# One core, transformer block: phi from v + 1, key sums out of G, normalized rows made by ScalarE

## The chip, the cores and the metric

The kernel runs on one core of a Trainium2 chip. The metric is device time in microseconds (us), the median of several executions. A core has TensorE (PE, the matrix engine), VectorE (DVE), ScalarE (ACT), GpSimd (POOL) and SyncE (SP), which here only starts DMAs. Each engine runs its own instructions in the order of the program and waits for the others through semaphores.

## The reference

The input x has 2048 rows of 512 numbers, all in float32.

```python
xn = layernorm(x)                                   # mean and variance of each row
q, k, v = split(xn @ wqkv)                          # 32 heads of 16
phi = lambda t: where(t > 0, t + 1, exp(t)) + 1e-6
pq, pk = phi(q), phi(k)
kv = einsum("bhsd,bhse->bhde", pk, v)               # per head 16 x 16
z = einsum("bhsd->bhd", pk)                         # per head 16: pk summed over all rows
o = einsum("bhqd,bhde->bhqe", pq, kv) / (einsum("bhqd,bhd->bhq", pq, z) + 1e-6)
s = o @ wo
g = silu((gelu(x @ w_gate) * (x @ w_up)) @ w_down)  # 1792 hidden columns; from x here: xn is not used
out = x + s * g
```

In the kernel the FFN and the attention read transposed operands that are made from the same 16 blocks of 128 rows.

## The kernel before

**Number format.** A float32 product is made of three TensorE passes over a high and a low half (`split`: ScalarE casts the high half, VectorE or GpSimd subtracts it to get the low one). The large products use a two by two scheme with seven products (names X, Y, Z in the attention, FX, FY, FZ and dX, dY, dZ in the FFN). One TensorE instruction is a 128x128 weight load and a 128x512 product.

**Stages.** The first stage takes the 16 blocks of x in eight pairs n = 0 to 7, `tokens[n]`. For a block, VectorE makes mean and variance (`bn_stats`, `bn_aggr`), GpSimd the reciprocal root (`rstd`, L557), then `xn` is made. For pairs 0 to 5 (`n < TX`, TX = 6) VectorE makes it (L573, `TENSOR_SCALAR`) and TensorE transposes it into PSUM (`pt`, L643). For pairs 6 and 7 ScalarE makes it (L565), it goes to DRAM (`xn_d`) and comes back laid out so (`xq`) that VectorE can transpose it (L617, `STREAM_TRANSPOSE`). Then come k and q of the block: `plain` products for pairs 0 and 1, the seven products for the others. `phi` (L703 to L713) is relu of -v and exp on ScalarE, and a VectorE operation. G = pk^T xn is summed over all blocks in four PSUM banks (`gps`), and v is never made: kv is G times the v columns of `wqkv` (`pkv`). The sum z of pk is kept by GpSimd (`zacc`, L722, one addition for each block) and summed over partitions by two TensorE products with ones (`pz`, L933); ScalarE copies it to `zq` (L940).

The second stage is the FFN in two halves of seven steps, each with the work on q's denominators and on q's transposes (`den`, `turn`) beside it. At the end stand the products `sps` of attention and output weights, and for each tile a VectorE product with silu's result, an addition of x, and a DMA out (`out_tile`). The last of these tiles is cut into two halves of 256 columns, each with its own product and DMA.

**What sets the order.** All operations are recorded (`do`), and the list `ORDER` gives the sequence in which they are issued, over all engines. It is one long list of numbers, made ahead of time; nothing is decided at run time. Tiles live in numbered places, so an operation that writes one waits for the readers of what was there.

**Idle products.** Twelve products `warm` of a constant tile stand ahead of everything on TensorE (`WARM`), and two more beside the first transposes.

Lines of the profile: L442 is TensorE's sum of passes, L398 and L400 a copy or cast on ScalarE or VectorE, L404 a two-operand operation on VectorE or GpSimd, L394 every DMA. Names tell these apart.

Of the kernel before, what the change touches and what calls it, by code (L numbers as in the profile page):

```python
# [288 lines left out]
def pool(n):  # L289
    return 0.18 + 0.0021 * n  # L290
# [3 lines left out]
def kernel(  # L294
# [246 lines left out]
    def load_next():  # L541
        if xq:
            load_x(xq.pop(0))

    xns = {}

    def ln(*ts):
        n = len(ts)
# [910 lines left out]
```

## Time and profile before

| what | before |
|---|---|
| median of 3 runs | 567.49 us (566.92 to 567.54) |
| the profiled execution | 566.9 us, span 564.8 us |
| PE busy | 557.8 us, 99% |
| DVE / ACT / POOL busy | 493.2 us / 360.8 us / 253.1 us |
| granted TensorE clock, mean | 0.999 |

The span runs from the first to the last instruction; 2.1 us of the profiled execution lie outside it. The ends of products are modelled by the profile, so a busy TensorE is told better by the distance of its starts.

### The profile page before, as it was taken

What the parts mean: (1) busy time and instruction counts of PE and PEld (TensorE: products, weight loads), DVE (VectorE), ACT (ScalarE), POOL (GpSimd) and SP (SyncE); (2) the same over time, 40 slices, a digit from 0 to 9 for tenths busy, and PEclk for the clock granted to TensorE, in tenths of its full rate; (3) what the DMA queues carried; (4) which work ended last, traced back from release to release, by engine and by line L of the source; (5) the groups of instructions that cost most, each with busy time, mean ns of one, the idle gap of its engine ahead of it and who ended that gap; (6) DMA issues with size and microseconds to landing.
All of it is one profiled execution on the core that took longest, in us unless ns stands there. A gap on an engine that the chain in (4) does not pass through costs nothing.

```text
span 564.8 us, 7902 instructions
## 1 busy us (share of the span) xinstructions
PE 557.8 (99%) x2630; PEld 487.0 (86%) x2630; DVE 493.2 (87%) x774; ACT 360.8 (64%) x668; POOL 253.1 (45%) x237
## 2 busy tenths in 40 slices
PE   8999999999999999999999999999999999999997
PEld 6888888888888888888888888888888888888886
DVE  7999999987798999999888776774889989898997
ACT  5987898877677876564536467867555636354730
POOL 4656677757786876431251940430413212314200
PEclk9999999999999999999999999999999999999999
DMA  7378967879978668158867998696757475778776
GB/s 266 104 217 273 274 203 233 255 223 322 352 241 300 240 234 339 43 201 311 265 233 216 389 339 335 239 344 254 243 187 242 173 247 194 233 228 286 239 247 239
DMA packets 78952, 141.29 MB, mean 250 GB/s; under 512 B 4672, under 2 KB 47680, under 8 KB 74944
## 3 DMA queue, kind: packets, MB, share of 16 engines
q1 hardware_dynamic: 78912, 140.79, 72.9%
q8 instruction: 21, 0.34, 0.2%
q14 instruction: 19, 0.16, 0.1%
HBM read 87.82 MB, written 52.95 MB: 249 GB/s over the span
## 4 chain that ended last, share of the span: by engine, by line
PE 91%; DVE 5%; DMA 2%; issue 1%; SPq 1%; ACT 0%; DVEq 0%; ACTq 0%
PE FX L442 26%; PE FZ L442 13%; PE dX L442 12%; PE gps L442 7%; PE FY L442 6%; PE dY L442 6%; PE X L442 6%; PE sps L442 4%; PE dZ L442 3%; PE Z L442 3%; PE q L442 2%; PE k L442 2%; PE Y L442 1%; DVE acc L1119 1%; PE pt L643 1%; DMA wk<-in_A_wqkv 1%
## 5 line engine op out<-in xcount | busy, mean ns | idle before, releaser
L442 PE MATMUL FX<-Xh,w 128*128 128x512 f32 x448 | 125.4, 379 | 0.0
L442 PEld LDWEIGHTS FX<-Xh,w 128*128 128x128 f32 x448 | 84.7, 189 | 12.0
L404 POOL TENSOR_TENSOR sums<-draw 128x256 f32<-128x256 f32 x28 | 26.5, 951 | 109.6 <-DVE dl L404 56.3
L1165 POOL TENSOR_TENSOR h<-h,g 128x512 f32<-128x512 f32 x28 | 39.5, 1411 | 65.9 <-DVE h L404 64.2
L442 PE MATMUL FX<-Xl,w 128*128 128x512 f32 x224 | 66.0, 379 | 0.0
L442 PE MATMUL FZ<-Xh,w 128*128 128x512 f32 x224 | 64.4, 379 | 0.0
L398 ACT COPY dY<-dX 128x512 f32<-128x512 f32 x56 | 32.1, 573 | 46.2 <-DVE acc L1119 28.4
L398 ACT COPY fu<-FX 128x512 f32<-128x512 f32 x56 | 32.7, 585 | 23.3 <-PE FX L442 19.4
L442 PEld LDWEIGHTS FX<-Xl,w 128*128 128x128 f32 x224 | 42.3, 189 | 6.0
L442 PEld LDWEIGHTS FZ<-Xh,w 128*128 128x128 f32 x224 | 42.3, 189 | 6.0
L398 ACT CAST hfh<-sums 128x512 fp32r<-128x512 f32 x56 | 34.5, 619 | 14.3 <-DVE sums L404 14.3
L442 PE MATMUL dX<-hfh,dh 128*128 128x512 f32 x112 | 41.9, 380 | 0.1
L442 PE MATMUL dX<-hfl,dh 128*128 128x512 f32 x112 | 41.5, 380 | 0.0
L442 PE MATMUL dX<-hfh,dl 128*128 128x512 f32 x112 | 41.0, 379 | 0.0
L1119 DVE TENSOR_TENSOR acc<-acc,dY 128x512 f32<-128x512 f32 x48 | 32.7, 681 | 8.9 <-PE dY L442 8.7
L404 DVE TENSOR_TENSOR hfl<-sums,hfh 128x512 fp32r<-128x512 f32 x56 | 40.2, 728 | 0.1
L404 POOL TENSOR_TENSOR tmp<-raw 128x256 f32<-128x256 f32 x28 | 29.1, 1049 | 20.1 <-DVE we L404 10.6
L1119 DVE TENSOR_TENSOR acc<-acc,dX 128x512 f32<-128x512 f32 x48 | 32.7, 683 | 5.5 <-PE dX L442 5.2
L960 POOL TENSOR_TENSOR qz<-qz,zq 128x512 f32<-128x512 f32 x16 | 23.3, 1456 | 23.1 <-DMA qz<-q_d 18.3
L442 PE MATMUL FY<-Xh,w 128*128 128x512 f32 x112 | 33.1, 379 | 0.0
L442 PE MATMUL FZ<-Xl,w 128*128 128x512 f32 x112 | 33.0, 379 | 0.0
L404 DVE TENSOR_TENSOR hfl<-h,hfh 128x512 fp32r<-128x512 f32 x42 | 32.2, 774 | 0.6 <-ACT hfh L398 0.6
(222 smaller groups left out, 1517.7 us busy)
## 6 DMA issues: line engine op xcount, KB each, us to landing
w<-w_d SPq DMA_DIRECT2D x17, 1792.0 KB, 7.9
w_d<-w SPq DMA_DIRECT2D x11, 1792.0 KB, 8.8
draw<-in_B_w_down SPq DMA_DIRECT2D x14, 512.0 KB, 4.0
w_d<-we SPq DMA_DIRECT2D x18, 256.0 KB, 2.2
x<-in_A_x SPq DMA_DIRECT2D x16, 256.0 KB, 3.3
q_d<-qp SPq DMA_DIRECT2D x16, 256.0 KB, 3.7
qz<-q_d SPq DMA_DIRECT2D x16, 256.0 KB, 3.1
q<-q_d SPq DMA_DIRECT2D x16, 256.0 KB, 3.8
```

What stands on the lines that cost most here:

```text
L398: do("ACT", act(n, src.psum), lambda o, i: nc.scalar.copy(o, i), dst, src, name=name)
L404: do(eng, c, lambda o, p, q: getattr(e, f"tensor_{op}")(o, p, q), dst, a, b, name=name)
L442: nc.tensor.matmul(o if r is None else o[:, r], a, turned(b), start=first, stop=made == self.passes[r], skip_group_check=self.on or r is n ...
L643: nc.tensor.transpose(o[:, k, :], a[:, j * P:(j + 1) * P], b)
L960: do("POOL", pool(D), lambda o, z: nc.gpsimd.tensor_mul(o, o, z.unsqueeze(1).to_broadcast([P, KT, P])), rows_of(q), zq, name="u")
L1119: do("DVE", dve(D), lambda o, i: nc.vector.tensor_add(o, o, i), o, ps, name="acc")
L1165: do("POOL", pool(NC), lambda o, i: nc.gpsimd.tensor_mul(o, o, i), h, g, name="h")
```

## The change

- **v + 1.** Where VectorE adds two partial products (`added`), it now adds 1 as well (`c` = v + 1). `phi` of such a tile is exp(c - 1) on ScalarE and max(min(exp, 1), c) on VectorE: one ScalarE operation instead of two, for 12 of the 32 tiles.
- **z.** VectorE writes 1 into the first column of each block of xn, once its transpose has been taken. Row 0 of G is then the sum of pk. It goes to DRAM (`z_d`), and four DMAs bring it to `zq`. `zacc` with its 16 additions, the products `pz` and ScalarE's copies are gone. As a row of xn sums to zero, the lost column is put back through the weights: row 0 of the v columns (`w0`) is subtracted from all of them, two 128x512 tiles on GpSimd and two on VectorE.
- **xn.** `TX` goes from 6 to 4: pairs 4 and 5 go through DRAM as 6 and 7 do. For pairs 1 to 3 (`XA`) ScalarE makes xn, which TensorE transposes as before. VectorE makes only that of pair 0.
- **Idle products.** Sixteen instead of twelve ahead of everything.
- **ORDER** is a new list.

```diff
-    988, 5, 0, 4, 7, 2, 10, 8, 11, 12, 9, 17, 6, 1, 18, 24, 16, 19, 20, 15, 28, 25, 13, 21, 29, 56, 62, 61, 63, 65, 116, 14, 57, 75, 117, 58, 118, 67,
...
-WARM = 12, 2
+WARM = 16,2
...
+    z_d = dram_view([1, D], "z_d")
...
+    neg_one = tile_in("sm", "no", [P, 1], F32, "neg_one")
+    do("DVE", 0.1, lambda o: nc.vector.memset(o, -1.0), neg_one, port=False)
...
-    TX = 6
+    TX = 4
...
+    XA = [(1, 5), (2, 6), (3, 7)]
...
+        if ts in XA:
+            nb = little("nb", f"nb{ts[0]}", [P, n])
+            do("DVE", 0.11, lambda o, i, r: nc.vector.scalar_tensor_tensor(o, i, -1.0, r, op0=ALU.mult, op1=ALU.mult),
+               nb, mv[:, :, 0], rstd)
         for i, t in enumerate(ts):
+            if ts in XA:
+                xns[t] = U("xn", range(4, 9), f"xn{t}")
+                v = xns[t].map(lambda ap: ap.rearrange("p (g q d) -> p q g d", g=KT, d=32))
+                do("ACT", 0.72, lambda o, i, r, b: nc.scalar.activation(o, i, AF.Identity, bias=b, scale=r),
+                   v, xs.pop(t).map(lambda ap: ap.rearrange("p (q g d) -> p q g d", q=KT, d=32)), rstd[:, i:i + 1], nb[:, i:i + 1], name=f"xn{t}")
+                xns[t] = xns[t], v
+                continue
...
+        do("DVE", 0.1, lambda o: nc.vector.memset(o, 1.0), (x[0] if isinstance(x, tuple) else x)[:, 0:1], name="one", port=False)
...
-        tt("DVE", "add", c, e, ps, D, name)
+        do("DVE", 0.6, lambda o, i, j: nc.vector.scalar_tensor_tensor(o, i, 1.0, j, op0=ALU.add, op1=ALU.add), c, ps, e, name=name)
...
+        if not v.psum:
+            do("ACT", act(D), lambda o, i, b: nc.scalar.activation(o, i, AF.Exp, bias=b), r, v, neg_one, name="exp")
+            p0 = U("p", range(24, 28), f"{nm}p{t}")
+            do("DVE", 0.6, lambda o, i, j: nc.vector.scalar_tensor_tensor(o, i, 1.0, j, op0=ALU.min, op1=ALU.max),
+               p0, r, v, name="phi")
+            return p0
...
-        do("POOL", pool(D), lambda o, i: nc.gpsimd.tensor_add(o, o, i), zacc, p0, name="zacc")
...
-    do("PE", 2 * PASS, run_z, pz, ones_r, *zs, key="z")
...
-    do("ACT", 0.7, turn_z, zq, pz, name="zb")
+    dma(z_d(0, slice(None)), GT[0][0:1], 2)
+    for k in range(KT):
+        dma(zq[32 * k:32 * k + 32].map(lambda ap: ap.rearrange("p (g d) -> p g d", d=32)),
+            z_d(0, slice(None)).map(lambda ap, k=k: ap.rearrange("o (g q d) -> o q g d", q=KT, d=32)[:, k].to_broadcast([32, KT, 32])), 16)
...
+    w0 = tile_in("up", 29, [P, D], F32, "w0")
+    dma(w0, ext(wqkv[0:1, 2 * D:3 * D].to_broadcast([P, D])), 256)
+    for c in range(KT):
+        tt("DVE" if c % 2 else "POOL", "sub", wv[c], wv[c], w0, D, "wv")
```

**VectorE at the start of the program.** `st` is a block's statistics, `mv` its mean and variance, `ve` the variance plus a constant. Before:

```order
L552 BN_STATS st_128<-x_97 128x6
L464 MEMSET neg_half 128x1
L553 BN_AGGR mv_133<-st_128 128x2
L555 TENSOR_SCALAR ve_139<-mv_133 128x1
L573 TENSOR_SCALAR xn_148<-x_97,mv_133,rstd_141 128x4x4x32
L552 BN_STATS st_152<-x_121 128x6
```

Now, with the second block's statistics ahead of the first block's xn:

```order
L554 BN_STATS st_133<-x_99 128x6
L555 BN_AGGR mv_136<-st_133 128x2
L557 TENSOR_SCALAR ve_141<-mv_136 128x1
L554 BN_STATS st_152<-x_125 128x6
L586 TENSOR_SCALAR xn_154<-x_99,mv_136,rstd_143 128x4x4x32
L555 BN_AGGR mv_157<-st_152 128x2
```

The block that these statistics read is the fourth DMA of the program, before and now.

**ScalarE at the start of the program**, from the first transposed block on. `kq` are the high halves of weights, `Xh` those of x, `wk` and `wq` the weights as they come from DRAM. Before:

```order
L398 CAST Xh_163<-pt_154 128x2x128 x2
L398 CAST kq_135<-wk_119 128x512
L398 CAST kq_135<-wk_113 128x512
L398 CAST b_0_207<-pt_196 128x256
L398 CAST Xh_163<-pt_196 128x2x128
L398 CAST kq_220<-wq_137 128x512
L398 CAST Xh_163<-pt_215 128x4x128
```

Now:

```order
L399 CAST Xh_172<-pt_161 128x2x128 x2
L399 CAST kq_186<-wq_131 128x512
L399 CAST kq_138<-wk_121 128x512
L399 CAST kq_138<-wk_123 128x512
L580 ACTIVATE xn_212<-x_127,nb_202,rstd_191 128x4x4x32
L580 ACTIVATE xn_217<-x_129,nb_202,rstd_191 128x4x4x32
L399 CAST Xh_172<-pt_207 128x2x128
L399 CAST kq_231<-wq_131 128x512
L399 CAST Xh_172<-pt_221 128x4x128
```

Two xn of pair 1 stand ahead of the cast of the second block, and a cast of `wq` ahead of the second half of `wk`.

**TensorE at the end of the program**, the last `sps` sums. Before:

```order
L442 MATMUL sps_5675<-pqh,Mh_4270 128x512 x2
L442 MATMUL sps_5812<-pqh,Ml 128x256 x4
L442 MATMUL sps_5800<-pqh,Mh_4075 128x256 x2
L442 MATMUL sps_5800<-pqh,Mh_4270 128x256 x2
L442 MATMUL sps_5800<-pqh,Mh_4075 128x256 x2
L442 MATMUL sps_5800<-pqh,Mh_4270 128x256 x2
L442 MATMUL sps_5812<-pqh,Mh_4075 128x256 x2
L442 MATMUL sps_5812<-pqh,Mh_4270 128x256 x2
L442 MATMUL sps_5812<-pqh,Mh_4075 128x256 x2
L442 MATMUL sps_5812<-pqh,Mh_4270 128x256 x2
```

Now:

```order
L443 MATMUL sps_5784<-pqh,Mh_4346 128x256 x2
L443 MATMUL sps_5784<-pqh,Mh_4566 128x256 x2
L443 MATMUL sps_5784<-pqh,Mh_4346 128x256 x2
L443 MATMUL sps_5784<-pqh,Mh_4566 128x256 x2
L443 MATMUL sps_5769<-pqh,Ml 128x512 x4
L443 MATMUL sps_5769<-pqh,Mh_4346 128x512 x2
L443 MATMUL sps_5769<-pqh,Mh_4566 128x512 x2
```

The last sum was a half tile of 256 columns and is now a whole tile of 512.

## Rows read from the trace of the kernel before

**Rows 1.** The page: busy time of the engines.
```profile
PE 557.8 (99%) x2630; PEld 487.0 (86%) x2630; DVE 493.2 (87%) x774; ACT 360.8 (64%) x668; POOL 253.1 (45%) x237
```
**Rows 2.** Stretches: busy us and count of each engine, granted clock, DMA share, GB/s.
```profile
5.50:6.70 1.20, 0.00 (x0) 0.00 (x0) 1.20 (x2) 0.53 (x1) 1.20 (x2) 1.00 1.05 362
10.50:40.00 29.50, 29.50 (x145) 25.38 (x144) 28.85 (x52) 26.03 (x50) 17.42 (x16) 1.00 0.55 168
40.00:130.00 90.00, 89.97 (x429) 78.33 (x428) 83.45 (x136) 75.35 (x142) 60.60 (x56) 1.00 0.80 242
```
**Rows 3.** Timeline of PE: start us, us, what, count (a pitch, a transposed tile, pz).
```profile
45.54 0.60 PE L643 MATMUL pt<-blk,xn 128*128 128x128 f32 x4
45.90 0.46 PE L442 MATMUL gps<-pkh,xnl 128*128 128x512 f32 x1
46.20 0.59 PE L442 MATMUL gps<-pkh,xnh 128*128 128x512 f32 x2
...
135.51 0.59 PE L933 MATMUL pz<-z,ones_r 128*128 128x512 f32 x2
135.95 0.59 PE L442 MATMUL FX<-Xh,w 128*128 128x512 f32 x2
```
**Rows 4.** Timeline of the start: VectorE, GpSimd, TensorE, the DMA queue (SPq).
```profile
1.11 4.37 PE L472 MATMUL warm<-blk 128*128 128x128 f32 x24 [1.11 <-DVE blk L462]
2.17 1.39 SPq L394 DMA_DIRECT2D x<-in_A_x  x3
3.42 0.69 DVE L552 BATCH_NORM_STATS2 st<-x 128x6 f32<-128x512 f32 x1 [2.36 <-DMA x<-in_A_x]
5.12 2.68 POOL L404 TENSOR_TENSOR kq<-wk,kq 128x512 fp32r<-128x512 f32 x2
5.19 1.48 DVE L573 TENSOR_SCALAR xn<-x,mv,rstd 128x512 f32<-128x512 f32 x1 [0.68 <-POOL rstd L557]
6.73 0.66 PE L643 MATMUL pt<-blk,xn 128*128 128x128 f32 x4 [1.25 <-DVE xn L573]
9.28 0.54 DVE L573 TENSOR_SCALAR xn<-x,mv,rstd 128x512 f32<-128x512 f32 x1
14.27 0.60 PE L643 MATMUL pt<-blk,xn 128*128 128x128 f32 x4
```
**Rows 5.** The fourth DMA alone (x): us from issue to landing.
```profile
DMA to landing us min/median/max: 3.9/3.9/3.9
```
**Rows 6.** Timeline of ScalarE: xn twice; a wait for TensorE.
```profile
98.17 1.52 ACT L565 ACTIVATE xn<-x,nb,rstd 128x512 f32<-128x512 f32 x2
99.59 0.62 ACT L708 ACTIVATE kr<-c 128x512 f32<-128x512 f32 x1
...
32.78 0.60 ACT L708 ACTIVATE qr<-q 128x512 f32<-128x512 f32 x1 [1.47 <-PE q L442]
```
**Rows 7.** Timeline of the end: a 512 wide tile, then two halves of 256.
```profile
558.69 0.68 DVE L1335 TENSOR_TENSOR acc<-acc,sps 128x512 f32<-128x512 f32 x1
558.91 1.95 PE L442 MATMUL sps<-pqh,Mh 128*128 128x256 f32 x16
559.40 0.69 DVE L404 TENSOR_TENSOR acc<-acc,sxr 128x512 f32<-128x512 f32 x1
560.90 0.42 DVE L1333 TENSOR_TENSOR acc<-acc,sps 128x256 f32<-128x256 f32 x1
561.35 0.42 DVE L404 TENSOR_TENSOR acc<-acc,sxr 128x256 f32<-128x256 f32 x1
```
**Rows 8.** DMAs out, issued at 560.1 (512 wide) and 561.8 (256 wide): landing.
```profile
DMA to landing us min/median/max: 2.5/2.5/2.5
...
DMA to landing us min/median/max: 1.9/1.9/1.9
```
**Rows 9.** Groups: line, engine, operation, shapes, count, busy us, mean ns, idle before.
```profile
L722 POOL TENSOR_TENSOR zacc<-zacc,kp 128x512 f32<-128x512 f32 x16 | 24.0, 1499 | 6.5 <-DVE kp L711 6.2 <-DVE mv L553 0.2
...
L1079 ACT ACT_TABLE_LOAD x3 | 3.8, 1283 | 0.0
```

More of the change, by code (lines that the diff above doesn't have):

```diff
@@ L464 @@
     do("DVE", 0.1, lambda o: nc.vector.memset(o, -0.5), neg_half, port=False)
+    neg_one = tile_in("sm", "no", [P, 1], F32, "neg_one")
+    do("DVE", 0.1, lambda o: nc.vector.memset(o, -1.0), neg_one, port=False)
     do("POOL", 0.8, lambda o: make_identity(nc, o), ident)
-    zacc = const("zacc", [P, D])
-    do("POOL", 0.6, lambda o: nc.gpsimd.memset(o, NT * EPS), zacc)
     den_eps = tile_in("sm", "de", [P, H // KT], F32, "den_eps")
@@ L922 @@
         GT.append(g)
-    pz = bank(7, "pz")
-    ones_r = tile_in("sm", "onr", [P, P], F32R, "ones_r")
-    do("ACT", 0.2, lambda o, i: nc.scalar.copy(o, i), ones_r, ones, name="ones")
-    zs = [tile_in("up", n, [P, D], F32R, f"z{n}") for n in (29, 32)]
-    split(*zs, zacc, D, "z")
-    def run_z(o, a, *zs):
-        for n, z in enumerate(zs):
-            nc.tensor.matmul(o, a, turned(z), start=n == 0, stop=n == 1)
-    do("PE", 2 * PASS, run_z, pz, ones_r, *zs, key="z")
-    zq = const("zq", [P, P])
-    def turn_z(o, i):
-        for k in range(KT):
-            rows = slice(32 * k, 32 * k + 32)
-            nc.scalar.copy(o[rows].rearrange("p (g d) -> p g d", d=32),
-                           i[rows].rearrange("p (g q d) -> p g q d", q=KT, d=32)[:, :, k])
-    do("ACT", 0.7, turn_z, zq, pz, name="zb")
+    zq = const("zq", [P, P])
+    dma(z_d(0, slice(None)), GT[0][0:1], 2)
+    for k in range(KT):
+        dma(zq[32 * k:32 * k + 32].map(lambda ap: ap.rearrange("p (g d) -> p g d", d=32)),
+            z_d(0, slice(None)).map(lambda ap, k=k: ap.rearrange("o (g q d) -> o q g d", q=KT, d=32)[:, k].to_broadcast([32, KT, 32])), 16)
     do("DVE", 0.2, lambda o, i: nc.vector.tensor_reduce(o, i, axis=AX.X, op=ALU.add), den_eps,
@@ L1379 @@
     g_take(100)
-    pe_keys += keys[2:5] + ["z"] + keys[5:KV] + [("kv", g) for g in range(KT)] + keys[KV:KV + 3]
+    pe_keys += keys[2:KV] + [("kv", g) for g in range(KT)] + keys[KV:KV + 3]
     pe_keys += [("m", g) for g in range(KT)] + keys[KV + 3:]
```

287 rows, old and new, of the table ORDER are left out of this document.

## The prediction

> **What bounds the kernel now.** I read the page's busy times first, then windows, then timelines of the three places that the change touches, and last the lone DMAs and groups. The busy times show TensorE at 557.8 of 564.8 us and VectorE at 493.2; ScalarE and GpSimd stand at 64% and 45% [rows 1]. The windows show how even that is: from 10.5 to 40 us TensorE is busy for all of the 29.5 us, from 40 to 130 for 89.97 of 90 [rows 2]. The reader is to see there, too, that the other engines are not equally free: in the first of these stretches ScalarE has 26.03 of 29.5 and VectorE 28.85, in the second VectorE has 83.45 of 90. TensorE is idle for a stretch of its own only at the start, between the last warm product (1.11 + 4.37 = 5.48) and the first transpose (6.73), which waits for VectorE's xn [rows 4]. So three things count: TensorE's work, which nothing covers; the time until TensorE runs without a gap; and the tail behind the last product.
>
> **TensorE's work.** A transposed tile is four instructions. In the timeline two products and one tile lie between 45.54 and 46.20: a tile, a gps product, and the next; less one product of 0.22 (135.51 to 135.95 holds two) the tile costs 0.66 - 0.22 = 0.44 [rows 3]. Pairs 4 and 5 go from TensorE to VectorE's transposes, four tiles: 4 x 0.44 = 1.76. The two pz products are gone: 0.44. Together 2.2 us. Both stood in stretches in which TensorE has no gap, so all 2.2 comes out of the time if the work ahead of it is ready; what is late next is ScalarE in the first 40 us (below). For the ends: 1.7, if the tiles are paid back by waits for xq, and 2.6 at the 0.6 that the profile models for one tile.
>
> **The warm products.** Four more of them, at 4.37 / 12 = 0.36 each (a mean over a cold and a warm part), end at 5.48 + 1.46 = 6.9. The first transpose cannot start before 7.3 (next step), so they cost nothing; if that step were as early as 6.73 they would cost 0.2.
>
> **The start.** The order shows the second block's statistics ahead of the first block's xn on VectorE. That x is the fourth DMA: issued at 2.17 [rows 4], landing 3.9 later [rows 5], at 6.07. The statistics take 0.69, so xn starts at 6.76 instead of 5.19. It then lasts 0.54 as at 9.28, with GpSimd quiet, or 1.48 as at 5.19, beside the two kq subtractions of GpSimd (5.12 to 7.80) [rows 4]. The second of these will still run then, until about 7.7. So xn ends between 7.3 and some 7.9, against 6.67, and the first transpose is 0.6 to 1.2 later.
>
> The row at 5.19 shows VectorE's xn at nearly three times its lone time beside GpSimd's kq [rows 4]. The Trainium skill, SBUF — State Buffer, section "Who interferes with whom", says that the port pair shared by VectorE and GpSimd is an exclusive lock, so that an instruction of VectorE that needs it does not start slowly but waits for the whole instruction of GpSimd. By that rule xn would end near 7.9, and without it at 7.3, which would take 0.6 off the term below.
>
> After that ScalarE sets the pace: its order has a cast of wq and the two of wk, then two xn of pair 1 ahead of the cast of the second block. An xn costs 0.71 there (98.17 to 99.59 holds two) [rows 6]. No row shows this sequence, so I estimate it: of the 7.5 us from the first transpose (6.73) to the tile at 14.27 [rows 4] some 4.4 are casts of ScalarE, waits for weights and the pair's statistics, which stay; the two xn add 1.4 ahead of the second block's cast. From a first transpose at about 7.7 that puts the second block's first product at about 13.5. How far that is behind I tell by the clock less the work done. Before, at the tile at 14.27 [rows 4], TensorE had done 20 products and three tiles: 20 x 0.216 + 3 x 0.44 = 5.6, so 8.6 of the clock had gone otherwise. Now at 13.5 the order has 11 products and four tiles behind TensorE, 4.1, so 9.4. The start costs 0.7 more. The ends: 0.2 less than before, if ScalarE's bias is early enough that the two xn fit beside the first block's products, and 1.5 more, if the 1.2 of the first transpose and a part of the xn add up. I take 0.7, which lies near the later transpose alone.
>
> **The tail.** The last sum was 256 wide: behind it an addition (560.90 to 561.35), another (0.42 and the issue) [rows 7], and a landing of 1.9 [rows 8]: 0.45 + 0.45 + 1.9 = 2.8. Now the last is 512 wide: 558.69 to 559.40, the same again [rows 7], and a landing of 2.5 [rows 8]: 0.71 + 0.71 + 2.5 = 3.9. That is 1.1 more. TensorE's products are the same in number of columns, and a half tile's two additions of before may still have stood in VectorE's queue; I take 0.95, with 0.5 and 1.5 as ends.
>
> **What lies beside other work.** ScalarE's relu goes for 12 tiles; each was queued with work of the same tile that VectorE still has to do, and TensorE has no gap there, so nothing is gained. GpSimd loses sixteen additions, 24.0 us [rows 9], at 45% busy: nothing. VectorE's xn go (ten) and its transposes, the columns of ones and w0's two subtractions come, about 2.5 us more over the first 140; its idle time of 6.5 between 40 and 130 [rows 2] holds that. If that cover were gone, up to 2.5 would show. The row of G goes through DRAM by DMAs that come back before the denominators are wanted; two landings, 5 us, lie beside FFN products; the bound is a wait of VectorE of 0 to 2.7, hidden while TensorE has FFN products queued, so 0. ScalarE loads its tables twice more, 1.28 each [rows 9], in a stage in which it is idle for long: 0. SP issues more DMAs in the first stage; what waits behind them in its queue is loads for later steps: 0, with 0.5 as the end.
>
> **Sum.** -2.2 + 0.7 + 0.95 = -0.55. On the profiled execution's 566.9 us (span 564.8 and 2.1 outside) that is 566.35; the median of the runs stands 0.59 above that execution, so 566.9.
>
> **The rivals.** A change below 0.2% (1.13 us) cannot be told from none by a measurement of this kernel.
>
> *The start and the tail are hidden, and TensorE's saving comes through.* For it: TensorE has no gap in 119.5 us [rows 2], and 2.2 us of its work are gone for certain. Against it: ScalarE's order puts two xn ahead of the second block. With 0 at the start and 0.5 at the tail: -2.2 + 0.5 = -1.7, 565.8.
>
> *ScalarE becomes the bound of the first 40 us; slower.* It gets six xn there, 6 x 0.71 = 4.26, and hands over only one small cast. From 10.5 to 40 it had 29.5 - 26.03 = 3.47 idle [rows 2], so it is over full by 0.8. And it has to wait for TensorE as well: if one wait as that of 1.47 at 32.78 [rows 6] stays, TensorE loses 0.8 + 1.5 = 2.3 behind it, on top of the start's 0.7: -2.2 + 0.7 + 2.3 + 0.95 = 1.75, 569.2. It decides from a loss of 1.7 on (1.13 + 0.55). Against it: these are the only extra instructions, and work can slide beyond 40 us, where ScalarE has 14.65 of 90 idle [rows 2].
>
> *TensorE's clock falls in the longer start.* The first stretch would be idle from 6.9 to 7.9, then hold 4.1 of work in the 5.6 us until 13.5. At 1.2 GHz that work takes 8.2, 2.7 more: -0.55 + 2.7 = 2.15, 569.6. Against it: before, the granted clock is 1.00 (2.4 GHz) even in 5.5 to 6.7, where TensorE does nothing [rows 2], and the new idle stretch is no longer. The Trainium skill, TensorE: Matmul & The Clock Gate, section "HAM oscillation — how this bites in real kernels", has a TensorE that is left waiting between bursts go back to 1.2 GHz; this trace's row shows none in its one gap.
>
> *The change doesn't do what it says.* The order shows the tiles and pz gone; without that saving the start and the tail alone would give +1.65, 569.1. One in a hundred.
>
> **How the numbers follow.** Forecast 0.41, the work comes through 0.33, ScalarE's bound 0.20, the clock 0.05, the last 0.01. The predicted time is the forecast's, 566.9; its own range is 566.4 to 568.6. The second case is faster by over 0.2% (565.8 against 566.36), the last three slower, the forecast within: 0.33, 0.41, 0.26. The range reaches down to 565.0 (-2.6 - 0.2 + 0.5 = -2.3, the three better ends, is 565.2) and up to 569.5, where ScalarE's bound with a little more than its price ends: 565.0 to 569.5.
>
> **What would show it.** Right: the first xn on VectorE starts near 6.8 and the first transpose lies between 7.3 and 8; at some 13.5 TensorE starts the second block and has no gaps of more than 0.3 up to 40 us; 16 transposes and pz fewer in the busy time; the last product some 1.2 earlier against the start's end than before, and a tail of 3.9 behind it. Wrong: gaps of TensorE that end on ScalarE's xn or the casts behind it between 13 and 40; a granted clock under 1.00 before 14; VectorE waiting for zq with TensorE idle beside it; a tail still at 2.8.

## The result and the profile after

The changed kernel takes 568.68 us in the median of 11 runs, the kernel before 567.49: a ratio of 1.0024, with a 95% interval of 1.0013 to 1.0035. A second set of runs gave 1.0021 (1.0010 to 1.0033). So the change makes it slower by about 1.3 us, where the forecast was 0.55 faster.

The profiled execution takes 568.7 us, its span is 566.7. First the page's busy times, in answer to [rows 1]:

```profile
PE 558.5 (99%) x2620; PEld 486.3 (86%) x2620; DVE 489.4 (86%) x791; ACT 359.9 (64%) x658; POOL 221.9 (39%) x222
```

TensorE has less work and yet is busy longer. The idle products count as busy, 6.70 us now and 4.37 before [rows 4], and the ends of products are modelled, so that the waits listed below add up to less than TensorE loses. The share of busy time tells nothing here. What tells is a column that I work out: the start of a product on the timeline less the pitches of all products and transposes ahead of it in TensorE's order (0.2157 for 512 columns, 0.1117 for 256, 0.11 for 128, as in one of a tile's four transposes; idle products not counted). Where that grows, TensorE lost time; it is good to about 0.1. In us:

| clock less work, first product behind | before | after | after, second profile |
|---|---|---|---|
| 14 us | 8.53 | 10.14 | 10.02 |
| 50 us | 8.81 | 10.36 | 10.26 |
| 140 us | 9.13 | 10.45 | 10.95 |
| 180 us | 9.23 | 12.00 | 11.75 |
| 340 us | 10.17 | 13.44 | 13.32 |
| the last product | 10.27 | 13.75 | 15.01 |
| work of all products | 550.42 | 548.23 | 548.23 |

Read downwards, the change in the first two columns is: the start +1.55, 50 to 140 us -0.23, behind 140 us +2.16, work -2.19. TensorE ends 1.29 later. The tail adds 0.6, and that is the span's 1.9.

The start, timeline of VectorE, GpSimd and TensorE, in answer to [rows 4]:

```profile
1.15 6.70 PE L473 MATMUL warm<-blk 128*128 128x128 f32 x32 [1.15 <-DVE blk L463]
7.12 0.69 DVE L554 BATCH_NORM_STATS2 st<-x 128x6 f32<-128x512 f32 x1 [2.39 <-DMA x<-in_A_x]
7.15 1.26 POOL L405 TENSOR_TENSOR kq<-wk,kq 128x512 fp32r<-128x512 f32 x1 [0.55 <-ACT kq L399]
7.73 0.97 DVE L586 TENSOR_SCALAR xn<-x,mv,rstd 128x512 f32<-128x512 f32 x1
8.76 0.44 PE L656 MATMUL pt<-blk,xn 128*128 128x128 f32 x2 [0.90 <-DVE xn L586]
```

VectorE waits 2.39 us for the fourth DMA, which lands at 7.1, 4.9 after its issue, and not at 6.07 [rows 5]. Only then come the first xn and, at 8.76 instead of 6.73, the first transpose.

ScalarE's stretch of 14 to 30 us (busy us of PE, PEld, DVE, ACT, POOL with counts, clock, DMA share, GB/s), of before and then of after:

```profile
14.00:30.00 16.00, 16.00 (x81) 13.76 (x81) 15.35 (x30) 14.67 (x30) 9.19 (x9) 1.00 0.35 105
```
```profile
14.00:30.00 16.00, 16.00 (x81) 13.80 (x80) 15.44 (x34) 15.94 (x33) 10.57 (x15) 1.00 0.55 165
```

ScalarE is full now, 15.94 of 16, and TensorE loses nothing by it: its clock less work grows by 0.22 from 14 to 50 us, before by 0.28.

TensorE's waits after, from the first transpose on (us in total, times, longest); before, no wait behind 16 us is listed:

```profile
PE pt L656 <- DVE xn L586: 0.9, 1, 0.9
PE k L443 <- ACT Xh L399: 0.6, 1, 0.6
PE dX L443 <- DVE acc L1129: 0.5, 1, 0.5
PE dY L443 <- ACT dY L399: 0.3, 1, 0.3
PE FY L443 <- ACT FY L399: 0.2, 1, 0.2
```

The last three stand in the FFN. One of them from the timeline of ScalarE and TensorE:

```profile
170.86 0.41 ACT L399 CAST dh<-draw 128x256 fp32r<-128x256 f32 x1 [0.83 <-DMA m_d<-m]
171.17 0.61 ACT L399 CAST hfh<-sums 128x512 fp32r<-128x512 f32 x1
171.69 0.58 ACT L399 COPY dY<-dX 128x512 f32<-128x512 f32 x1
172.33 0.48 PE L443 MATMUL dY<-hfh,dh 128*128 128x512 f32 x1 [0.27 <-ACT dY L399]
...
173.24 0.57 ACT L399 COPY FY<-FX 128x512 f32<-128x512 f32 x1
...
173.87 0.70 PE L443 MATMUL FY<-Xl,w 128*128 128x512 f32 x2 [0.20 <-ACT FY L399]
```

ScalarE stands 0.83 us before a cast of w_down's block (`dh`); the copies that TensorE needs for its next bank are queued behind it, and TensorE waits twice. In the list of before the first of these copies stands ahead of that cast, and neither of the two waits:

```profile
169.68 0.59 ACT L398 COPY dY<-dX 128x512 f32<-128x512 f32 x1
170.19 0.40 ACT L398 CAST dh<-draw 128x256 fp32r<-128x256 f32 x1
```

The end, timeline of TensorE and VectorE, in answer to [rows 7]:

```profile
561.12 1.03 PE L443 MATMUL sps<-pqh,Mh 128*128 128x512 f32 x4
562.19 0.69 DVE L1345 TENSOR_TENSOR acc<-acc,sps 128x512 f32<-128x512 f32 x1 [0.19 <-PE sps L443]
562.91 0.69 DVE L405 TENSOR_TENSOR acc<-acc,sxr 128x512 f32<-128x512 f32 x1
```

The last product ends at 561.98 (548.23 + 13.75), the last addition at 563.60, the span at 566.7: 1.62 and 3.10. Before it was 560.69, 561.77 and 564.8: 1.08 and 3.03.

### The profile page after: what moved, and what is told of

It is laid out like the page before. It is cut to its first block, busy times and chain, and to the rows that moved or that the text cites. A ratio compares the mean times of both kernels' runs of the same rounds, so it can differ in the third digit from the quotient of the medians.

```text
span 566.7 us, 7936 instructions
## 1 busy us (share of the span) xinstructions
PE 558.5 (99%) x2620; PEld 486.3 (86%) x2620; DVE 489.4 (86%) x791; ACT 359.9 (64%) x658; POOL 221.9 (39%) x222
## 4 chain that ended last, share of the span: by engine, by line
PE 92%; DVE 3%; DMA 2%; ACT 1%; POOL 0%; SPq 0%; issue 0%; DVEq 0%; POOLq 0%; ACTq 0%
PE FX L443 24%; PE dX L443 12%; PE FZ L443 12%; PE gps L443 7%; PE dY L443 6%; PE FY L443 6%; PE sps L443 6%; PE X L443 5%; PE dZ L443 3%; PE Z L443 3%; PE k L443 2%; PE q L443 2%; PE Y L443 1%; DMA x<-in_A_x 1%; DMA qz<-q_d 1%; PE pt L656 1%
## 5 line engine op out<-in xcount | busy, mean ns | idle before, releaser
L443 PE MATMUL FX<-Xh,w 128*128 128x512 f32 x448 | 128.4, 380 | 0.0
L1175 POOL TENSOR_TENSOR h<-h,g 128x512 f32<-128x512 f32 x28 | 38.2, 1363 | 103.0 <-DVE h L405 94.7
L405 POOL TENSOR_TENSOR tmp<-raw 128x256 f32<-128x256 f32 x28 | 27.3, 988 | 55.6 <-DVE w L405 19.3
L405 DVE TENSOR_TENSOR hfl<-sums,hfh 128x512 fp32r<-128x512 f32 x56 | 43.0, 775 | 3.9 <-ACT hfh L399 3.9
L443 PE MATMUL dX<-hfh,dl 128*128 128x512 f32 x112 | 42.3, 381 | 0.0
L405 DVE TENSOR_TENSOR hfl<-h,hfh 128x512 fp32r<-128x512 f32 x42 | 36.0, 863 | 1.4 <-PE dX L443 1.4
L399 ACT CAST hfh<-h 128x512 fp32r<-128x512 f32 x42 | 25.8, 618 | 14.2 <-PE dX L443 9.3
```

What stands on the lines that cost most here:

```text
L399: do("ACT", act(n, src.psum), lambda o, i: nc.scalar.copy(o, i), dst, src, name=name)
L405: do(eng, c, lambda o, p, q: getattr(e, f"tensor_{op}")(o, p, q), dst, a, b, name=name)
L443: nc.tensor.matmul(o if r is None else o[:, r], a, turned(b), start=first, stop=made == self.passes[r], skip_group_check=self.on or r is n ...
L1175: do("POOL", pool(NC), lambda o, i: nc.gpsimd.tensor_mul(o, o, i), h, g, name="h")
```

## The experiments

All ratios are to the kernel before, run on the same chip. Two lists of order are mixed in some: every operation keeps its data and its waits, only its place in the lists changes.

**The control.** The changed kernel again.

> The changed kernel once more, as the control for the others. TensorE's clock less its work was 10.36 us at 50 us in its first profile, 10.45 at 140, 12.00 at 180, 13.44 at 340 and 13.75 at its last product (before: 8.81, 9.13, 9.23, 10.17, 10.27). If these waits belong to the kernel, all five come back within 0.3 and the time is 1.0 to 1.5 us over before; if the FFN's waits were an accident of one execution, 180 and 340 stand elsewhere.

569.1 us, 1.0021 (1.0010 to 1.0033). The start came back within 0.1 and the waits at 171 to 177 us too (0.8). Behind 300 us it lost 1.5 at 310 to 320 and 1.7 behind 340, against 0.8 at 325 and 0.3 behind 340 in the first profile. The places move from one execution to the next; behind 140 us it is 3.3 and 4.1 in all, before 1.14. The mean granted clock is 0.997 to 1.000 in all 21 runs of the changed kernel, and 1.000 in the slowest of them (571.33 us): the clock is not what makes it slower.

**The first xn ahead of the second block's statistics**, in the changed kernel:

```diff
-    ..., 29, 14, 13, 56, 21, 25, 57, 116, ...
+    ..., 29, 14, 13, 21, 56, 25, 57, 116, ...
```

> The changed kernel with one pair of VectorE's instructions exchanged: the first block's xn ahead of the second block's statistics, as before. Theory (the statistics' wait for the fourth DMA makes the start late): the first transpose moves from 8.76 to near 7, the clock less the work at 50 us from 10.4 to about 9.0, and the time falls by 1.0 to 1.6 us. Rival (ScalarE's queue, with two xn ahead of the second block's cast, sets the start): the first transpose is earlier, but the clock less the work at 50 us stays at 10.0 to 10.4 and the time changes by under 0.4.

567.89 us, 1.0011 (0.9997 to 1.0024): 1.2 less than the control, though the two intervals overlap. The timeline of the start:

```profile
5.30 1.26 POOL L405 TENSOR_TENSOR kq<-wk,kq 128x512 fp32r<-128x512 f32 x1
5.37 1.48 DVE L586 TENSOR_SCALAR xn<-x,mv,rstd 128x512 f32<-128x512 f32 x1 [0.67 <-POOL rstd L559]
7.07 0.70 DVE L554 BATCH_NORM_STATS2 st<-x 128x6 f32<-128x512 f32 x1 [0.22 <-DMA x<-in_A_x]
7.32 0.38 PE L656 MATMUL pt<-blk,xn 128*128 128x128 f32 x2
```

The clock less work at 50 us is 9.34 instead of 10.26. Two instructions that changed places cost 0.9 of the 1.55; the two xn on ScalarE, which the rival blamed, stand where they did. The price isn't the same in every execution: in the six profiles that have 16 idle products and the new list from the start to at least 135 us, the fourth DMA lands 3.7 to 5.2 after its issue, the first transpose stands between 8.04 and 9.01, and the clock less work at 50 us between 9.7 and 10.65.

**The old order from 135 us on**, under the new operations:

```diff
-    ..., 810, 881, 875, 807, 1102, 1261, 884, 1097, ...
+    ..., 810, 881, 875, 803, 807, 811, 888, 889, ...
```

> The changed kernel's operations, in its own order up to the copies of G (about 135 us), and from there on in the order of the kernel before, with the new operations of z and w0 at their places. Theory (the z that comes through G and DRAM makes VectorE late, so TensorE waits in the FFN): the 2.2 us of waits between 140 and 400 us stay, or grow, as the v products now stand where w0's subtractions are not yet done. Rival (the new list orders the FFN worse, whatever z does): the waits fall to the 1.0 us of before, and the time by about 1 us; the tail falls by 0.5 under both.

575.73 us, 1.0152 (1.0125 to 1.0178). TensorE's longest wait, and GpSimd's between 130 and 150 us:

```profile
PE FZ L443 <- DVE g L405: 7.4, 1, 7.4
```
```profile
POOL qz L966 <- DMA zq<-z_d: 3.6, 1, 3.6
POOL wvo L405 <- DMA wvo<-in_A_wqkv: 1.1, 1, 1.1
```

In the old order the denominators are asked for before z has come back from DRAM; VectorE stands for them, and a product of the FFN behind it. So z by that way is some us later, and the new list had made room for it. TensorE's clock falls too, 4.6 us into this wait (139.1 to 146.5), so the time holds more than the wait:

```profile
144.00:150.00 6.00, 3.25 (x11) 2.78 (x12) 3.60 (x5) 1.29 (x3) 5.92 (x7) 0.50 0.45 138
```

From 150 us on, though, this kernel's clock less work grows by 1.16 (20.12 to 21.28), near the 1.05 of before, which speaks for the rival's list.

**z undone**, in the new order:

```diff
-    z_d = dram_view([1, D], "z_d")
+    zacc = const("zacc", [P, D])
...
-        do("DVE", 0.1, lambda o: nc.vector.memset(o, 1.0), (x[0] if isinstance(x, tuple) else x)[:, 0:1], name="one", port=False)
...
+        do("POOL", pool(D), lambda o, i: nc.gpsimd.tensor_add(o, o, i), zacc, p0, name="zacc")
...
+    do("PE", 2 * PASS, run_z, pz, ones_r, *zs, key="z")
...
-        tt("DVE" if c % 2 else "POOL", "sub", wv[c], wv[c], w0, D, "wv")
```

> The changed kernel with the change of z undone (GpSimd's sums, the two products and ScalarE's copies are back, no column of ones, no w0), all other operations in the new order. Theory (late z): TensorE's waits between 140 and 180 us (1.55) fall below 0.5, its work grows by 0.44, the time falls by about 0.7 to 1.1. Rival (the list): waits between 140 and 340 stay at 2.5 to 3, and the time rises by about 0.4.

583.49 us, 1.0279 (1.0258 to 1.0301), as neither theory has it. TensorE's waits:

```profile
PE pt L657 <- ACT xn L581: 3.0, 2, 2.6
PE gps L442 <- DVE pkl L740: 2.7, 4, 1.1
```

GpSimd's sixteen sums of 1.5 us [rows 9] went back to the places they had had in GpSimd's old queue, between operations that now stand otherwise. That they hold up the first 140 us (clock less work 23.44 there) is argued and not shown. The kernel says nothing about the FFN's waits: a part can't be undone alone under a list made for the whole.

**The old order from 217 us on:**

```diff
-    ..., 1684, 1544, 1363, 1652, 1649, 1961, 1651, ...
+    ..., 1684, 1544, 1363, 1409, 1410, 1649, 1651, ...
```

> The changed kernel with its own list up to about 217 us (z, the v products and the first denominators are then done) and the order of the kernel before from there to the end. Theory (behind 217 us the new list itself makes TensorE wait, and its last sum the tail): the waits after 220 us, 1.7 to 3.2 in the two profiles of the changed kernel, fall to the 1.0 of before, the tail shrinks by 0.55, and the time falls by 1.3 to 2.5 us. Rival (what the new operations left over, late sums on VectorE and tile places, makes these waits whatever the order): they stay at 1.7 or more, and only the tail's 0.5 is gained.

566.59 us, 0.9985 (0.9974 to 0.9995). From 220 us to the last product the clock less work grows by 1.04 (after 1.73 and 3.24, before 1.02). The operations are those of the changed kernel, so the list makes these waits. The end is two halves of 256 again.

**Both mended**, the start and the list from 217 us on:

```diff
-    ..., 29, 14, 13, 56, 21, 25, 57, 116, ...
+    ..., 29, 14, 13, 21, 56, 25, 57, 116, ...
...
-    ..., 1684, 1544, 1363, 1652, 1649, 1961, 1651, ...
+    ..., 1684, 1544, 1363, 1409, 1410, 1649, 1651, ...
```

> As the last, and the first block's xn ahead of the second block's statistics. If the two are independent their gains add: clock less work 9.3 at 50 us and about 11.5 at the end, the time 2.3 to 3.4 us under the changed kernel, which is 1 to 2 under the kernel before. If the start's gain is only slack that the FFN takes back, it is no faster than the last.

565.45 us, 0.9966 (0.9953 to 0.9978). 9.02 at 50 us, 11.06 at the end: the gains add (3.65 less than the control, where the two alone give 1.2 and 2.5).

**z's four DMAs in a row**, in the changed kernel; 980 to 982 are the second to the fourth:

```diff
-    ..., 1194, 1137, 979, 891, 1012, 894, 1132, ...
+    ..., 1194, 1137, 979, 980, 981, 982, 891, 1012, 894, 1132, ...
```

> The changed kernel with the four DMAs that bring z to zq issued in a row behind z_d, ahead of four loads of weights that stood between them. Theory (z is late for VectorE, and that makes TensorE wait at 171 to 177 us): VectorE's wait of 1.3 to 2.0 us at 141 goes, and TensorE's waits between 140 and 180, 0.8 to 1.55, fall below 0.4; the time falls by 0.5 to 1. Rival (those waits belong to the order of VectorE's work behind it, not to the z): the wait at 141 goes, TensorE's stay; the loads held back may cost up to 1 us at the v products.

568.3 us, 1.0011 (0.9996 to 1.0026). VectorE's wait for z between 135 and 150 us in the control was this, and is gone:

```profile
DVE den_eps L949 <- DMA zq<-z_d: 2.0, 1, 2.0
```

Between 140 and 180 us TensorE's clock less work grows by 0.14 only, as the theory has it. But in this execution it had grown by 0.9 between 50 and 140, nearly all of it at 63 us, long before z is made (the control by 0.7), and the time's interval overlaps the control's, so a gain isn't shown. The next run puts the theory to the test where TensorE comes earlier.

**All three mended**, the lists of the last two together:

```diff
-    ..., 29, 14, 13, 56, 21, 25, 57, 116, ...
+    ..., 29, 14, 13, 21, 56, 25, 57, 116, ...
...
-    ..., 1194, 1137, 979, 891, 1012, 894, 1132, ...
+    ..., 1194, 1137, 979, 980, 981, 982, 891, 1012, ...
...
```

> The changed kernel with all three pieces of order mended: the first xn ahead of the second statistics, z's four DMAs in a row, the order of the kernel before from 217 us on. Theory (three separate causes): the clock less the work is about 9.0 at 50 us, rises by under 0.3 between 140 and 200 (0.78 without z's DMAs in a row), and ends near 10.5; the time is 0.5 to 0.8 under the 565.45 of the kernel with two pieces mended, near 564.8. Rival (z's row of DMAs holds loads back, or the FFN takes the slack back later): 565.2 to 566.

565.85 us, 0.9958 (0.9941 to 0.9974), which the interval does not tell from the kernel with two pieces mended. Its waits between 140 and 200 are 0.72 against 0.78: they are there though z is no longer late. The late z can be a part of the control's waits, but it is not what makes these.

**The old order from 155 us on**, and the start mended, z's DMAs as in the new list:

```diff
-    ..., 29, 14, 13, 56, 21, 25, 57, 116, ...
+    ..., 29, 14, 13, 21, 56, 25, 57, 116, ...
...
-    ..., 1317, 1030, 1286, 1169, 1313, 1437, 1050, ...
+    ..., 1317, 1030, 1286, 1169, 1014, 1015, 1017, ...
```

> The changed kernel with the first xn ahead of the second statistics, and the order of the kernel before from about 155 us on in place of 217. If the waits of TensorE at 170 to 177 (0.75 in the kernel mended from 217 on) belong to the list's order there, they go and the time is about 0.5 to 0.8 less, near 564.8. If they follow from z and the v products being later than before, they stay at 0.5 or more, or others come in their place.

564.74 us, 0.9954 (0.9939 to 0.9970): 2.6 less than the kernel before, and the lowest median here, though the interval overlaps that of the kernel mended from 217 us on. TensorE's waits in its span are these four, all in the first 16 us:

```profile
PE warm L473 <- DVE blk L463: 1.2, 1, 1.2
PE k L443 <- ACT Xh L399: 0.6, 1, 0.6
PE pt L656 <- DVE xn L586: 0.4, 1, 0.4
PE k L443 <- DVE Xl L405: 0.3, 1, 0.3
```

From 160 us to the end the clock less work grows by 1.05 (9.46 to 10.51); before it was 1.05 (9.22 to 10.27). From 140 us it is 1.34 against 1.14. With the same operations, and z as late as in the changed kernel, all but 0.2 of the 2.16 that was lost behind 140 us is gone: the new list's order had made it.

**The old order of the last 120 operations:**

```diff
-    ..., 3487, 3513, 3496, 3443, 3574, 3497, 3446, ...
+    ..., 3487, 3513, 3496, 3434, 3443, 3520, 3528, ...
```

> The changed kernel with only the last 120 operations in the order of the kernel before: the last sum is two halves of 256 columns again. The profile after has 1.62 us from TensorE's last product to VectorE's last addition, the one before 1.07, and 3.1 and 3.0 from there to the end: so 0.5 to 0.6 us less is expected. By the prediction's term (0.95) it would be 0.5 to 1.5; by the rival that VectorE's queue sets the end anyway, nothing.

570.4 us, 1.0049 (1.0035 to 1.0062). The seam of the two lists itself cost TensorE 2.17 between 540 and 555 us. Behind the last product the tail is 1.29 to VectorE's end and 3.0 to the span's (565.52, 566.81, 569.8), 0.4 less than after. The size is settled, the kernel as a whole shows no gain.

**Twelve idle products** in the changed kernel:

```diff
-WARM = 16,2
+WARM = 12, 2
```

> The changed kernel with 12 idle products in place of 16 and nothing else. The prediction has them cost nothing, as the first transpose waits for xn (8.6 to 8.8) and the idle products end at 7.5 to 7.9: the time stays within 0.4 of the changed kernel. The rival, that a TensorE left idle from 6 to 8.7 falls to 1.2 GHz, gives a granted clock under 1.00 or products at twice their pitch behind 8.7, and up to 2 us more.

572.08 us, 1.0067 (1.0050 to 1.0084), 2.6 to 3 us over the control. Windows of its start (the clock is the third number from the right):

```profile
2.50:3.00 0.50, 0.50 (x4) 0.50 (x3) 0.00 (x0) 0.00 (x0) 0.00 (x0) 1.00 1.03 401
...
4.50:5.00 0.50, 0.50 (x7) 0.50 (x6) 0.19 (x2) 0.38 (x1) 0.20 (x1) 1.00 0.90 324
...
6.50:7.00 0.50, 0.00 (x0) 0.00 (x0) 0.50 (x2) 0.00 (x0) 0.50 (x2) 1.00 0.97 340
...
8.00:8.50 0.50, 0.35 (x2) 0.35 (x3) 0.50 (x3) 0.00 (x0) 0.00 (x0) 0.50 1.02 381
...
12.00:13.00 1.00, 1.00 (x4) 0.73 (x3) 1.00 (x4) 1.00 (x3) 0.00 (x0) 0.50 0.02 6
...
16.00:20.00 4.00, 4.00 (x22) 3.57 (x21) 3.12 (x8) 4.00 (x10) 2.67 (x4) 1.00 0.15 56
```

TensorE is idle from 5.66 to 8.15, and its granted clock is 0.50 (1.2 GHz) from 7.9 to 14.7 us. The mean granted clock is 0.992 to 0.997 in all ten runs. The clock less work at 50 us is 12.29, 2.0 more than the control's. The rival that I gave one chance in twenty happens here; in the changed kernel the four products keep it off.

**Twelve idle products with all three pieces mended:**

> The same with 12 idle products ahead of everything in place of 16. With xn early, the first transpose stood directly behind the last idle product (7.25, xn done at 6.8). If the sixteen products are what it waits for now, it moves to 6.9 and the time falls by 0.3 to 0.5; if they keep the clock up they are worth their time: then the first products run at half their pace and the time is the same or up to 1 longer.

565.77 us, 0.9964 (0.9950 to 0.9978), the same. The first transpose comes at 5.87 and not 7.29, and at 50 us only 0.24 of that is left.

**The one exchange in the kernel before**, statistics ahead of xn:

```diff
-    ..., 28, 25, 13, 21, 29, 56, 62, 61, ...
+    ..., 28, 25, 13, 56, 21, 29, 62, 61, ...
```

> The kernel before with one exchange on VectorE: the second block's statistics ahead of the first block's xn, as the change has it. If this pair alone makes the start late, the first transpose goes from 6.7 to 7.4 to 8.7 and the clock less the work at 50 us from 8.8 to 9.5 to 10; the time rises by 0.7 to 1.2. If TensorE falls to 1.2 GHz in the longer idle stretch (it has 12 idle products), it rises by 2 or more.

570.53 us, 1.0057 (1.0038 to 1.0076). Timeline and windows of its start:

```profile
6.88 0.69 DVE L552 BATCH_NORM_STATS2 st<-x 128x6 f32<-128x512 f32 x1 [2.10 <-DMA x<-in_A_x]
7.49 0.97 DVE L573 TENSOR_SCALAR xn<-x,mv,rstd 128x512 f32<-128x512 f32 x1
8.52 0.66 PE L643 MATMUL pt<-blk,xn 128*128 128x128 f32 x4 [1.95 <-DVE xn L573]
```
```profile
9.00:10.00 1.00, 0.89 (x7) 0.66 (x6) 0.96 (x6) 0.79 (x3) 0.57 (x1) 0.91 0.94 361
10.00:11.00 1.00, 1.00 (x3) 0.87 (x3) 0.96 (x4) 0.90 (x2) 0.50 (x1) 0.50 0.99 371
```

One pair of instructions makes the first transpose 1.8 later, and here, with 12 idle products, the clock falls as well: 11.57 at 50 us, +2.8, and 3.2 us in the time. The fourth DMA lands 4.7 after its issue, at 6.86, though this kernel's DMAs up to it are those of the kernel before, where it took 3.9.

**Sixteen idle products in the kernel before**, and **v + 1 alone in the kernel before:**

```diff
-WARM = 12, 2
+WARM = 16, 2
```
```diff
-        tt("DVE", "add", c, e, ps, D, name)
+        do("DVE", 0.6, lambda o, i, j: nc.vector.scalar_tensor_tensor(o, i, 1.0, j, op0=ALU.add, op1=ALU.add), c, ps, e, name=name)
...
+        if not v.psum:
+            do("ACT", act(D), lambda o, i, b: nc.scalar.activation(o, i, AF.Exp, bias=b), r, v, neg_one, name="exp")
```

> The kernel before with 16 idle products in place of 12. By the prediction's term for a transpose that is ready at 6.7 they cost 0.2; at the pace of 4 records in 0.5 us, which they kept in the kernel after, they end at 7.4 to 7.8 and cost 0.5 to 1.0, unless work behind them is held by the weights anyway.

> The kernel before with one part of the change alone: v + 1 out of VectorE's sums and one ScalarE operation in phi for 12 tiles, in the old order. The prediction has this worth nothing, since TensorE has no gap there: within 0.4 us of the kernel before. The rival, that ScalarE's relu stood in the chain to G's products, gives 0.5 to 1 us less.

567.71 us, 1.0006 (0.9995 to 1.0018), and 567.81 us, 0.9996 (0.9986 to 1.0006): both nothing that can be measured. In the first the transpose is 0.44 later (7.17), and from 14 us on only 0.02 of that is left; v + 1 takes 12 operations off ScalarE and TensorE does not end earlier for it.

## Why the prediction was wrong, point by point

The forecast was -0.55 and the profiled execution shows +1.8. The step that failed is the one at its very beginning, "So three things count: TensorE's work, which nothing covers; the time until TensorE runs without a gap; and the tail behind the last product.". There was a fourth: the new list itself, in stretches of the FFN in which the change touches no operation. I looked at the order only where operations came or went, and wrote "TensorE has no gap there" of a list that would not run any more. After the change TensorE waits 2.16 us more behind 140 us, and with the old list there 0.2. Of the 2.4 between forecast and measurement the list is 2.16 and the start 0.85; 50 to 140 us gave 0.23 back, and the tail came out 0.34 under its term.

The sign of this is shown better than the size. Behind 220 us the clock less work grows by 1.0 to 1.65 in the ten profiles that have the order of before there (the kernel before and three variants of it, six variants of the changed kernel), and by 1.7 to 3.3 in the five that have the new list to the end (the kernels with z undone and with the seam at the last 120 operations left aside). Which ScalarE and VectorE operations stand in the wrong place is shown for the wait at 172 us alone.

- **TensorE's work, -2.2.** Right: 550.42 to 548.23, and in the best kernel it comes out of the time whole (2.0 of the span, 2.6 of the median). The rows that the 0.44 of a tile was read from hold one tile and one product, not two products; the value stands.
- **The start, +0.7.** The mechanism was right, the size was off: +1.55. The fourth DMA was taken with its landing of one execution of before, 3.9; after the change it took 4.9. The new list isn't shown to be the cause: in the three other kernels that have the first DMAs of before it took 4.5, 4.6 and 4.7, and under the new list 3.6 to 5.2. The statistics' wait moved xn to 7.73 and not 6.76, and the load for GpSimd's second kq was late as well. Where the landing was 4.1 (z's four DMAs in a row), the start costs 0.87, near the 0.7. What was missing is the spread of a landing on which the whole start now hangs.
- **xn beside GpSimd.** By the Trainium skill's page "SBUF — State Buffer", section "Who interferes with whom", xn would wait for the whole instruction of GpSimd. The traces agree in part: xn ended behind kq, but only 0.29 behind (8.70 and 8.41), where all of its own 0.54 [rows 4] would come behind it by the rule.
- **ScalarE as the bound of the first 40 us.** The place was filled nearly as reckoned (15.94 of 16 from 14 to 30, 29.27 of 29.5 from 10.5 to 40), and nothing followed: 0.22 of growth between 14 and 50 us, before 0.28. A full ScalarE did not become a wait of TensorE. That this rival's time, 569.2, lies near the measured 568.7 is chance.
- **The idle products, 0.** Their cost was right (0.02 at 50 us in the kernel before), though they ended at 7.85 and not at 6.9. What they save was left out: without them the changed kernel loses 2 us at the start by the clock. The Trainium skill, "TensorE: Matmul & The Clock Gate", section "HAM oscillation — how this bites in real kernels", has a TensorE that waits between bursts go back to 1.2 GHz. The row at 8.0 of that kernel, 0.50 behind an idle stretch, agrees.
- **The clock's rival.** In the changed kernel's profiles the granted clock stays at 1.00, as forecast; with 12 idle products, or with the exchange in the kernel before, it falls. The price, 2.7, compares with the 2.0 that 12 idle products cost at the start (the 2.8 of the exchange holds the later transpose too). The idle stretch of 1 us behind 16 products was right in length (0.91, 7.85 to 8.76), but I did not ask what 12 would leave: 2.5.
- **The tail, +0.95.** +0.61: the additions cost 0.54 more, the landing 0.07 and not 0.6. From the last addition to the span's end it is 2.9 to 3.1 in all these kernels but the one with z undone (3.6), whatever the width.
- **Costs hidden off the path.** v + 1 gains nothing, as said. VectorE's wait for z was 1.3 to 2.0, inside the 0 to 2.7 given. In the kernel mended from 155 us on it is 2.1, and TensorE doesn't feel it there.

The operations of the change are worth -2.6 us with the order mended at the start and from 155 us on. In the list that came with them they cost +1.3.

## What to carry to other kernels

When a change comes with a new order of everything, the order is a part of the change of its own: compare it everywhere, or measure the new operations under the old order where it can still run. Follow each early instruction to the DMA it waits for; an in-order engine that takes the second block's load ahead of the first block's work hangs the first on that load's landing, and this landing moved between 3.6 and 5.2 us here. What keeps an engine awake has a price in its own time and another in what happens without it.

## What the runs showed of the hardware that was not expected

The granted clock of TensorE fell to 1.2 GHz in three kernels: at 7.9 us with 12 idle products in the changed kernel (idle since 5.66), at 9.8 with the exchange in the kernel before (idle from 6.57 to 8.52, then at work), and at 143.7 with the old order from 135 us on (idle since 139.1). It stayed there for 3.4 to 6.8 us though TensorE was back at work before it rose again. Behind 1.25 us [rows 2, 4] and behind 0.9 after the change it stayed at 2.4 GHz.

At the very start the rows grant 1.00 while the idle products come at 4 records in 0.5 us, and at 7 later (2.5 and 4.5 in the rows of the kernel with 12 of them). The trace's first record of the clock is the rise to 1.00, at 4.46 us there, at 4.14 in the kernel before and at 7.20 after; ahead of it a row prints 1.00 without a record, and the products' pace tells more.

VectorE's xn that starts beside a GpSimd subtraction ends 0.27 to 0.29 behind it wherever the two stand: 6.85 behind 6.56 with xn moved forward, 8.70 behind 8.41 after, 8.46 behind 8.19 with the exchange in the kernel before.

The same DMA, the fourth of the program, landed 3.6 to 5.2 us after its issue in the kernels here, also between kernels whose DMAs up to it are the same.

Not settled: why the places of the FFN's waits behind 300 us move between executions of the same list, and where the slowest run of the changed kernel, 571.33, lost its time; it has no trace.
